# Width transforms in groups of three, and b1 loaded through GpSimd's queue, in a GFNet plus GELU layer

## The chip, the core and the metric

The kernel runs on one core of one Trainium2 chip. The metric is the device time of one execution in microseconds; the time given for a kernel is the median over its runs.

## The reference

An input x of 2048 rows and 640 columns is normalised along its rows. The normalised x feeds two branches, and the input and both branches are added:

```python
def _A_ref(x, w_r, w_i):
    X = rfft2(x.astype(float32), axes=(-2, -1))
    X = X * (w_r + 1j * w_i)
    return irfft2(X, s=(S, D), axes=(-2, -1)).astype(bfloat16)

def _B_ref(x, w1, b1, w2, b2):
    h = gelu(einsum("bsd,df->bsf", x, w1) + b1)      # F = 1536
    return einsum("bsf,fd->bsd", h, w2) + b2

xn = _layernorm(x, axis=-1)
return x + _A_ref(xn, ...) + _B_ref(xn, ...)
```

Branch A is a global filter in the frequency domain, branch B a two-layer perceptron. All tensors are bfloat16.

## The kernel before

**Tiling.** Rows are dealt into 16 blocks of 128 (block c holds every sixteenth row, from row c). The transform over the 2048 rows is split into a transform over the 128 rows of each block (matmuls with the table `gtab`, the "height transforms") and one over the 16 blocks (table `mtab` forward, `ntab` back). The transform over the 640 columns uses symmetries: VectorE folds each row twice (L654, L658), and what is left are four products of 160 columns per block with the table `etab`. On the way back the table is `getab`, and VectorE unfolds twice (L887, L892).

**Stages.** Each stage is a set of operations with the engines they may run on:
- Load x; statistics (L595, L597), reciprocal root on GpSimd (L605), normalise (L619). Blocks 0 to 5 are transposed by TensorE (L631), the others by DMA (L642, on SP's queue).
- First layer of B: for each of seven sets of blocks (`BLOCKS`, 128 to 512 rows wide) and each of twelve chunks of F, five matmuls from `xnT` and W1 into a bank named `hps`, then a gelu on ScalarE (L693), which adds b1 as a column, `b1col`. That column is made from the loaded row of b1 by one matmul (L577) and one copy (L579).
- Forward: the height transforms, evicted to `XW`; then `along_d`, the transforms along the width, for a group of blocks at a time (`BPS`: pair at which the group is issued, first block, number of blocks), evicted to `Xb`, a ring of `NP` blocks; then, for each of eight pairs, the matmuls with `mtab`, evicted to `Y`; the product with the filter on VectorE (`T`, L786; `Z`, L791); small gathers `Zs`; the matmuls with `ntab`, evicted to `XV`.
- Second layer of B for the six `STAGED` blocks, whose sums with b2 are kept in float (L868); for the others it is accumulated in the bank of the final product.
- Back: transforms along the width with `getab` in groups `EPS`, unfolding, then the final matmuls with the table H (kept in `gtab`), the sum with x and b2 (L917) and the store (L920). x is added by accumulating DMAs that GpSimd issues (L906).

**One group of the width transforms** (`five`): each block has four main matmuls on 128 rows of contraction and four remainder matmuls on 32 rows. A group of m blocks issues main matmuls, then all remainders, then the rest of the main ones. A group of three writes two pairs of PSUM banks; a group of four writes a third pair, for its fourth block, and orders two remainders by a semaphore on TensorE itself. Eviction is one copy of 960 columns per pair, and one of 640 for the fourth block.

**Order.** A planner (`Sched.schedule`) walks through time with its own estimates of durations (`five_us`, `IPC` and the like), priorities (`PRIO`), allowed PSUM banks (`ZONE`), and gates, and fixes the order on every engine and queue, the engine of each copy, and the banks. The result is five lists, one for each engine and for SP; each engine runs its list in order and waits on semaphores where the planner found a dependency or a reused buffer. A small change of an estimate or a zone therefore moves many instructions. `QUEUE` is the order of the first loads on SP; `GATE`, `DEPTH` hold later loads back; `PARTS` cuts W1 and W2 by chunks of F: chunks 0 to 2 of W1 go through ScalarE's queue, the others through SP's.

**Lines to know.** Matmuls all carry L491 (transposes L631, the one for b1 L577). Copies from PSUM carry L501 on ScalarE and L504 on VectorE. All loads carry L482. `ps<-etab,XW` is a forward width transform, `ps<-getab,XV` one on the way back, `ps<-Xb,mtab` a forward column group, `ps<-ntab,Z` an inverse one, `ps<-xnT,W` the first layer, `ps<-W,gT` the second, `ps<-Wf,gtab` and `ps<-T,gtab` the final products.

Of the kernel before, what the change touches and what calls it, by code (L numbers as in the profile page):

```python
# [98 lines left out]
def mm_us(n):  # L99
    return max(n / 2400.0 + 0.003, 0.0265)  # L100


def dve_us(n, rate=1.0):
    return 0.066 + n / 960.0 / rate


def act_us(n, ptr=0):
    return 0.052 + n / 1200.0 + 0.092 * ptr
# [3 lines left out]
    return 0.075 + n / 500.0  # L112


ZONE = {'hps': ((4, 8), (0, 4), (2, 8), (2, 8), (0, 4), (4, 8), (0, 8)), 'bps': (0, 8), 'cps': (0, 8), 'dps': (0, 8), 'eps': (0, 6), 'fps': (0, 8), 'fst': (0, 8), 'yps': (0, 2), 'tps': (2, 6), 'aps': (0, 8)}
PRIO = {'hps': 1, 'gelu': 361.0, 'pb': 171.1, 'pc': 177.3, 'filt': 322.7, 'ipc': 497.3, 'xb': 65.8, 'eps': 262.2, 'fin': 110.8, 'fst': 95.7}
BLOCKS = ((0, 1), (1, 2), (2, 4), (4, 6), (6, 9), (9, 12), (12, 16))
AHEAD = 3
STAGED = (0, 2, 4, 6, 8, 10)
XRAT = 4  # L120
LAG = 6
WARM = 11
DEPTH = 5
PACE = 5
BYDMA = (6, 7, 8, 9, 10, 11, 12, 13, 14, 15)
PARTS = (0, 3, 8, 12)
BPS = {0: (0, 4), 1: (4, 4), 3: (8, 4), 5: (12, 4)}
EPS = (0, 3, 6, 10, 13, 16)
NP = 8
W1RATE = 360000.0  # L130
GATE = 2
QUEUE = (('x', 0), ('x', 1), ('w', 1), ('x', 2), ('w', 2), ('x', 6), ('x', 4), ('g', 0), ('x', 10), ('x', 12), ('x', 8), ('x', 14))
XGATE = -16


# [265 lines left out]
def bass_parallel_sum__spectral_gfnet__dense_activation_gelu__prompt_kernel(  # L401
# [17 lines left out]
    b1v = B_b1.rearrange("(c p) -> c p", p=128)  # L419
    b2v = B_b2.rearrange("(o e) -> o e", o=1)  # L420

    K = Sched(nc, ["sp", "pe", "act", "dve", "pool"])
    with ExitStack() as es:
        def sb(name, shape, dtype=BF):
            return es.enter_context(nc.sbuf_tensor(name, shape, dtype))

        def view(t, off, dims):
            width = int(np.prod(t.shape[1:]))
            return bass.AP(tensor=t, offset=off, ap=[[width, 128]] + dims)
# [8 lines left out]
        b1t = sb("b1t", [NFC, 128])  # L438
# [12 lines left out]
        Wf = sb("Wf", [128, WP])  # L451
        xb4 = sb("Xb", [128, 2 * NP * KP])
        Yb = sb("Y", [128, 2, 4 * KP])
# [27 lines left out]
        def load(dst, src, buf, nbytes, after=(), reads=(), rate=330e3, eng="sp", cost=0.46, lat=0.0):  # L481
            return K.op([(eng, cost)], 400 if eng == "act" else 0, lambda e, _: e.dma_start(dst, src), reads=reads, writes=[buf], after=after, nbytes=nbytes, rate=rate, lat=lat)  # L482
# [3 lines left out]
        def mms(lst):  # L486
            def f(e, _):
                for o_, lw, rh, st, sp_, *mark in lst():
                    if mark == ["wait"]:
                        e.wait_ge(fence, len(fences))  # L490
                    ins = e.matmul(o_, lhsT=lw, rhs=rh, start=st, stop=sp_)  # L491
                    if mark == ["signal"]:
                        ins.then_inc(fence, 1)
                        fences.append(ins)
                return ins
            return f
# [12 lines left out]
        K.op([("pool", 0.1)], 100, lambda e, _: e.memset(mhalf[:, 0:8], -0.5), writes=[B_mh])  # L509
        K.op([("pool", 0.1)], 99, lambda e, _: e.memset(view(xb4, KP - 2, [[2 * KP, NP], [1, 3]]), 0.0), writes=[B_xbpad])  # L510
        K.op([("pool", 0.1)], 99, lambda e, _: e.memset(view(xb4, 2 * KP - 1, [[2 * KP, NP], [1, 1]]), 0.0), writes=[B_xbpad])
        wpad = K.op([("pool", 0.1)], 99, lambda e, _: e.memset(view(Wf, 2 * WR, [[1, 2]]), 0.0), writes=[B_wpad])


        B_id, B_b1, B_b2b = Buf("ident"), Buf("b1t"), Buf("b2")
# [12 lines left out]
        def load_w1(j, **how):  # L528
            a, n = PARTS[j], PARTS[j + 1] - PARTS[j]
            load(view(W1, D * a, [[128 * n, 5], [1, 128 * n]]), w1v[:, :, 128 * a:128 * (a + n)], B_w1s[j], 163840 * n, rate=W1RATE, **how)  # L530
# [4 lines left out]
        late_x = []  # L535
        for what, i in QUEUE:
            if what == "x":
# [4 lines left out]
                load(gtab[:].rearrange("p a b -> p (a b)"), const["G"], B_g, 524288)  # L542
        load(ident[:], const["I"], B_id, 32768, eng="act")
        load_w1(0, eng="act")
        load(b1t[:], b1v, B_b1, 3072, eng="act", lat=-3.0)
        few = []

        later = [load(etab[:], const["E"], B_e, 204800), load(mtab[:].rearrange("p a b c d -> p (a b c d)"), const["M"], B_m, 131072),
# [58 lines left out]
        for c in range(16):  # L607
            pr, prf = 100 - c, 100 - c - LAG
            if c % 2 == 0:
# [15 lines left out]
            if c not in BYDMA:  # L625
                for ja, jb, engs in ((0, 5, "da"),) if c > 1 else ((0, 3, "d"), (3, 5, "a")):
                    tps = Buf(f"tps{c}_{ja}", psum, 1, ZONE["tps"])

# [32 lines left out]
            for c in (c - 1, c):  # L661
                aps = Buf(f"aps{c}", psum, 2, ZONE["aps"])
                ring_ops.append(K.op([("pe", 5 * mm_us(128))], prf, mms(lambda c=c, xfv=xfv, aps=aps: [
# [17 lines left out]
        for blk, (c0, c1) in enumerate(BLOCKS):  # L681
            s0, s1 = 128 * c0, 128 * c1
            for fc in range(NFC):
                hps = Buf(f"hps{blk}_{fc}", psum, 1, ZONE["hps"][min(blk, len(ZONE["hps"]) - 1)])
                B_gT[blk, fc] = Buf(f"gT{blk}_{fc}")
                pr = PRIO["hps"] - blk - fc / 20
                part = []
                for js in ((0, 1, 2), (3, 4)):
# [3 lines left out]
                hps_ops.setdefault(blk, []).append(part[0])  # L692
                K.op([("act", act_us(s1 - s0, 1))], pr + PRIO["gelu"], lambda e, _, s0=s0, s1=s1, fc=fc, hps=hps: e.activation(  # L693
                    gT[:, fc, s0:s1], ps(hps.slot, 0, s1 - s0), ACT.Gelu_apprx_tanh, bias=b1col[:, fc:fc + 1], scale=1.0),
# [38 lines left out]
            return PS[buf.slot // 2][:, :].rearrange("p (b n) -> p b n", b=2)[:, :, 0:2 * Q4].rearrange("p b (g k) -> p b g k", g=2)  # L733

        def five_us(m):
            return 4 * m * 0.0695 + m * 0.07 + 0.21
        IPC = 0.78
        pb_ops, filt_ops, cps_ops, t_ops = [], [], {}, {}
        B_v = [Buf(f"v{q}") for q in range(16)]
        B_xb = {}  # L740
# [1 line left out]
        def along_d(i0, m, gate):  # L742

            assert i0 % NP + m <= NP
            bps = [Buf(f"bps{i0}_{v}", psum, 2, ZONE["bps"]) for v in range(2 + m // 4)]
            pr = PRIO["pb"] - i0 / 10
            pb_ops.append(K.op([("pe", five_us(m))], pr, mms(lambda: five(
                bps, lambda g, n: Xa[:, g, i0 + n, :], lambda g, n: Xa[32 * g:32 * g + 32, 4, i0 + n, :], etab, m)),
                reads=B_xa + [B_e], writes=bps, gate=gate))
            free = [o for i in range(max(0, i0 - NP), i0 + m - NP) for o in cps_ops[i // 2]]  # L750
            for i in range(i0, i0 + m):
                B_xb[i] = Buf(f"xb{i}")
            for v in range(2):
                K.op([("dve", dve_us(2 * Q4 * min(m, 3))), ("act", act_us(2 * Q4 * min(m, 3)))], pr,
                     copy(lambda v=v: view(xb4, (i0 % NP) * 2 * KP + v * (KP + 1), [[2 * KP, min(m, 3)], [1, 2], [2, Q4]]),
                          lambda v=v: two(bps[v], min(m, 3))), reads=[bps[v]], writes=[B_xb[i] for i in range(i0, i0 + min(m, 3))], after=free)
# [4 lines left out]
        for pair in range(8):  # L761
            if pair in BPS:
                along_d(BPS[pair][0], BPS[pair][1], cps_ops.get(pair - 2, []))
            Y, TB, Z = Buf(f"Y{pair}", p_y), Buf(f"T{pair}", p_t), Buf(f"Z{pair}", p_z)
            cps = [Buf(f"cps{pair}_{r}", psum, 2, ZONE["cps"]) for r in range(2)]
            cps_ops[pair] = [K.op([("pe", 0.78)], PRIO["pc"] - pair / 5, mms(lambda pair=pair, cps=cps: [
                (ps(cps[r].slot + hi, 0, KP)[64 * qq:64 * qq + 64], mtab[64 * hi:64 * hi + 64, 1 if pair == qq == 0 else 0, v, r, :],
                 view(xb4, (2 * (2 * pair % NP + qq) + v) * KP, [[1, KP]])[64 * hi:64 * hi + 64], v == 0, v == 1)
                for r in range(2) for v in range(2) for hi in range(2) for qq in range(2)]), reads=[B_xb[2 * pair], B_xb[2 * pair + 1], B_xbpad, B_m], writes=cps, gate=t_ops.get(pair - 2, []))]
            for r in range(2):  # L770
                K.op([("act", act_us(644)), ("dve", dve_us(644))], PRIO["pc"] - pair / 5,
                     copy(lambda Y=Y, r=r: view(Yb, Y.slot * 4 * KP + r * KP, [[2 * KP, 2], [1, KP]]),
# [8 lines left out]
            def tv(TB, k, r):  # L781
                return view(TT, TB.slot * 8 * KP + k * 4 * KP + r * KP, [[2 * KP, 2], [1, KP]])
            pr = PRIO["filt"] - pair / 5
            t_ops[pair] = []
# [22 lines left out]
            for n in range(2):  # L807
                gather((128 * n + 31, [[256, 2], [1, 1]]), (KP * n, [[2 * KP, 2], [1, 1]]), 1.0 - 2 * n, tail[n:n + 1], [("dve", 0.07), ("act", 0.06)])
            dps = [Buf(f"dps{pair}_{hi}", psum, 2, ZONE["dps"]) for hi in range(2)]

            def ipc(pair=pair, Z=Z, ZS=ZS, zs=zs, dps=dps):
# [16 lines left out]
                return lst  # L828
            K.op([("pe", IPC)], PRIO["ipc"] - pair / 5, mms(ipc), reads=[Z, ZS, B_n], writes=dps)
            for hi in range(2):  # L830
# [14 lines left out]
        def fin_gate(c):  # L845

            i = rest.index(c)
            return ([fin_ops[rest[i - AHEAD]]] if i >= AHEAD else st_ops[:]) + hps_ops[block_of[c]]

# [15 lines left out]
        for i, c in enumerate(STAGED):  # L865
# [3 lines left out]
                out=halves(view(xnT, 2 * D * i, [[1, 2 * D]]).bitcast(F32)), in0=ps2(fps.slot, H2), in1=halves(b2bc[:]), op=ALU.add), reads=[fps, B_b2b], writes=[B_st2[c]], after=all_hps)  # L869
        for e, (c0, c1) in enumerate(zip(EPS, EPS[1:])):  # L870
            m = c1 - c0
# [24 lines left out]
            for n in range(m):  # L896
# [11 lines left out]
                for pcs in (WHOLE,) if c < 15 else (((0, 0, H2),), ((0, H2, H2 + Q4),), ((0, H2 + Q4, D),)):  # L908
                    a, b = pcs[0][1], pcs[-1][2]
                    os_, fps = Buf(f"os{c}_{a}", p_os), Buf(f"fps{c}_{a}", psum, len(pcs), ZONE["yps" if c in STAGED else "fps"])  # L910
# [42 lines left out]
```

## Time and profile before

| | |
|---|---|
| median of 4 runs | 153.57 us (153.42 to 155.1) |
| the profiled execution | 153.62 us, span of its instructions 151.7 us |
| TensorE busy | 147.1 us, 97% of the span |
| VectorE, ScalarE, GpSimd busy | 114.9, 85.0, 21.0 us |
| granted TensorE clock | 1.0 |
| moved by DMA | 20.81 MB, 137 GB/s over the span |

The profile is one execution. Times in its lines are microseconds from the start of the span; a timeline line gives the start, the time to the end of the last instruction of the row, the engine, the line of the program, the operation, the tiles (out<-in), their shape, the number of instructions, and in brackets the idle time of the engine before the row and what ended it. Ends of matmuls are modelled, so that neighbouring rows overlap; the distance between two starts is what a row costs TensorE. PE is TensorE's matmul, PEld its loading of weights, DVE VectorE, ACT ScalarE, POOL GpSimd.

### The profile page before, as it was taken

How to read it: one execution, taken by the hardware profiler on the slowest of the kernel's cores; microseconds unless marked ns; L12 is line 12 of the kernel's file. 1: busy time of each engine (PE TensorE's matmuls, PEld its weight loads, DVE VectorE, ACT ScalarE, POOL GpSimd, SP SyncE). 2: the span in 40 equal slices, each digit the busy share in tenths (PEclk: the TensorE clock that was granted, in tenths of full speed). 3: DMA queues.
4: the chain of work that ended last, by engine and by line, in shares of the span. 5: the costliest groups of instructions: out<-in, count | busy, mean ns of one | idle time of the engine just before them, and what ended most of it. 6: DMA issues, size and time to landing. Idle time of an engine off the chain costs nothing.

```text
span 151.7 us, 3730 instructions
## 1 busy us (share of the span) xinstructions
PE 147.1 (97%) x1547; PEld 101.6 (67%) x1547; DVE 114.9 (76%) x251; ACT 85.0 (56%) x172; POOL 21.0 (14%) x33
## 2 busy tenths in 40 slices
PE   7899999999999999999999999999999999999993
PEld 2399999956666656546456775677677777777773
DVE  1888999999996599679759838984896597594232
ACT  3297978877778677967974416685403461211000
POOL 1202112110100000000000132058202202212000
PEclk9999999999999999999999999999999999999999
DMA  4999235889697550220605052439955715743511
GB/s 126 367 375 399 98 40 141 190 195 206 104 170 164 102 180 0 57 77 0 201 20 179 0 122 56 86 85 198 236 135 155 194 43 123 192 121 97 139 67 49
DMA packets 20120, 20.81 MB, mean 137 GB/s; under 512 B 8328, under 2 KB 16776, under 8 KB 19976
## 3 DMA queue, kind: packets, MB, share of 16 engines
q1 hardware_dynamic: 16976, 14.81, 36.0%
q0 software_dynamic: 2304, 5.24, 15.8%
q10 hardware_dynamic: 824, 0.53, 1.1%
q8 instruction: 12, 0.20, 0.6%
q14 instruction: 4, 0.03, 0.1%
HBM read 13.69 MB, written 2.62 MB: 108 GB/s over the span
## 4 chain that ended last, share of the span: by engine, by line
PE 85%; ACT 5%; DMA 5%; DVE 2%; SPq 1%; POOL 1%; issue 0%
PE ps L491 84%; DMA XV<-in_A_x_dram 5%; ACT Xb L501 3%; DVE stats L595 1%; ACT gT L693 1%; PE ps L631 1%; SPq L482 1%; ACT XV L501 1%; ACT Zs L501 1%; POOL rstd L605 1%; DVE T L619 0%; DVE T L658 0%; DVE ost L917 0%; DVE mv L597 0%; DVE ve L604 0%
## 5 line engine op out<-in xcount | busy, mean ns | idle before, releaser
L491 PE MATMUL ps<-xnT,W 128*128 128x128 bf16 (+3 forms) x420 | 56.8, 288 | 0.1
L491 PE MATMUL ps<-W,gT 128*128 128x320 bf16 (+1 forms) x396 | 56.9, 295 | 0.0
L491 PEld LDWEIGHTS ps<-W,gT 128*128 128x128 bf16 x396 | 37.4, 98 | 14.4 <-issue 0.5
L491 PEld LDWEIGHTS ps<-xnT,W 128*128 128x128 bf16 x420 | 34.0, 98 | 15.5 <-ACT gT L693 2.9
L693 ACT ACTIVATE gT<-ps,b1col 128x128 bf16<-128x128 f32 (+3 forms) x84 | 40.2, 505 | 6.9 <-PE ps L491 5.6
L501 ACT ACTIVATE XW<-ps 128x640 bf16<-128x640 f32 (+1 forms) x17 | 13.5, 812 | 8.4 <-PE ps L491 8.0
L904 ACT ACTIVATE xo<-b2bc 128x640 f32<-128x640 bf16 x10 | 7.1, 732 | 16.1 <-DVE ost L917 16.1
L595 DVE BATCH_NORM_STATS2 stats<-XV 128x6 f32<-128x320 bf16 x32 | 14.1, 469 | 2.7 <-DMA XV<-in_A_x_dram 2.7
L917 DVE TENSOR_TENSOR ost<-ps,xo 128x640 bf16<-128x640 f32 (+2 forms) x12 | 8.5, 710 | 8.5 <-PE ps L491 8.5
L906 POOL DMA_DIRECT2D xnT<-in_A_x_dram x6 | 6.3, 1050 | 60.9 <-DVE xnT L868 60.9
L504 DVE CAST XW<-ps 128x640 bf16<-128x640 f32 (+1 forms) x10 | 9.2, 922 | 5.6 <-PE ps L491 5.6
L786 DVE TENSOR_TENSOR T<-Y,Wf 128x1288 bf16<-128x1288 bf16 x16 | 12.8, 825 | 0.3
L906 POOL DMA_DIRECT2D xo<-in_A_x_dram x10 | 8.8, 954 | 25.8 <-ACT xo L904 25.7
L501 ACT ACTIVATE Xb<-ps 128x960 bf16<-128x960 f32 (+1 forms) x7 | 7.4, 1096 | 5.9 <-PE ps L491 5.9
L605 POOL TENSOR_TENSOR rstd<-ve,mhalf 128x2 f32<-128x2 f32 (+1 forms) x9 | 6.3, 705 | 31.3 <-DVE ve L604 31.3
L504 DVE CAST Xb<-ps 128x960 bf16<-128x960 f32 (+1 forms) x5 | 5.8, 1174 | 5.0 <-PE ps L491 5.0
L504 DVE CAST XV<-ps 128x640 bf16<-128x640 f32 x8 | 6.6, 821 | 3.6 <-PE ps L491 3.6
L501 ACT ACTIVATE Y<-ps 128x644 bf16<-128x644 f32 x9 | 6.3, 706 | 5.0 <-PE ps L491 4.8
L501 ACT ACTIVATE Zs<-Z 128x128 bf16<-128x128 bf16 (+1 forms) x32 | 6.5, 278 | 2.1 <-DVE Z L791 2.1
L501 ACT ACTIVATE XV<-ps 128x640 bf16<-128x640 f32 x8 | 5.6, 705 | 3.6 <-PE ps L491 3.6
L504 DVE CAST Y<-ps 128x644 bf16<-128x644 f32 x7 | 5.8, 824 | 2.4 <-PE ps L491 2.4
L491 PE MATMUL ps<-getab,XV 128*128 128x160 bf16 (+1 forms) x128 | 7.6, 232 | 0.0
(53 smaller groups left out, 138.9 us busy)
## 6 DMA issues: line engine op xcount, KB each, us to landing
xo<-in_A_x_dram POOLq DMA_DIRECT2D x10, 320.0 KB, 4.6
out_dram<-ost SPq DMA_DIRECT2D x15, 160.0 KB, 2.1
XV<-in_A_x_dram SPq DMA_DIRECT2D x7, 320.0 KB, 9.7
xnT<-in_A_x_dram POOLq DMA_DIRECT2D x6, 320.0 KB, 3.8
W<-in_B_w_dram SPq DMA_DIRECT2D x2, 800.0 KB, 5.8
W<-in_B_w_dram SPq DMA_DIRECT2D x2, 640.0 KB, 6.3
Wf<-in_A_w_r_dram SPq DMA_DIRECT2D x7, 160.5 KB, 3.2
Wf<-in_A_w_i_dram SPq DMA_DIRECT2D x7, 160.5 KB, 4.0
```

The lines of the kernel that those rows point to most:

```text
L482: return K.op([(eng, cost)], 400 if eng == "act" else 0, lambda e, _: e.dma_start(dst, src), reads=reads, writes=[buf], after=after, nbyte ...
L491: ins = e.matmul(o_, lhsT=lw, rhs=rh, start=st, stop=sp_)
L501: return e.activation(dst(), src(), ACT.Copy, scale=scale)
L504: return e.tensor_copy(dst(), src())
L595: K.op([("dve", 0.4)], 100 - c, lambda e, _, c=c, h=h: e.bn_stats(stats[:, c, 6 * h:6 * h + 6], view(XV, c * D + H2 * h, [[1, H2]])), read ...
L605: K.op([("pool", 0.75)], 100 - c, lambda e, _, a=a, b=b: e.tensor_tensor(out=rstd[:, a:b], in0=ve[:, a:b], in1=mhalf[:, 0:b - a], op=ALU.pow),
L631: ins = e.transpose(ps(tps.slot, 0, 512).bitcast(BF)[:, 128 * j:128 * j + 128], xnv(128 * j, [[1, 128]]), ident[:])
L693: K.op([("act", act_us(s1 - s0, 1))], pr + PRIO["gelu"], lambda e, _, s0=s0, s1=s1, fc=fc, hps=hps: e.activation(gT[:, fc, s0:s1], ps(hps. ...
L786: t_ops[pair].append(K.op([("dve", 0.05 + dve_us(4 * KP, 2))], pr, lambda e, _, k=k, Y=Y, TB=TB, pair=pair: e.tensor_tensor(out=view(TT, T ...
L904: K.op([("act", act_us(640))], 30, lambda e, _, xov=xov: e.activation(xov(0, D), b2bc[:], ACT.Copy), reads=[B_b2b], writes=[xi], gate=[z_l ...
L906: K.op([("pool", 1.2)], 50, lambda e, _, c=c, xov=xov: e.dma_start(xov(0, D), xv[:, c, :], accum_op=ALU.add), reads=[xi], writes=[xo], nby ...
L917: os_ops.append(K.op([("dve", dve_us(b - a))], 95, lambda e, _, a=a, b=b, xov=xov, fps=fps, os_=os_: e.tensor_tensor(out=ost[:, os_.slot, ...
```

## The change

The forward width transforms are issued as five groups of three blocks and one group of one (blocks 0-2, 3-5, 6-8, 9-11, 12-14, and 15) instead of four groups of four. The ring of `Xb` holds six blocks instead of eight. On the way back the groups are of 3, 3, 3, 4, 3 blocks instead of 3, 3, 4, 3, 3, so that one group of four is left in the kernel. The row of b1 is loaded by GpSimd's queue instead of ScalarE's, where it stood behind the first part of W1. The planner's priorities, zones and lags are new, its estimates for a group of four and for an inverse group are larger, and two loads of x change places with others in the queue.

```diff
-ZONE = {'hps': ((4, 8), (0, 4), (2, 8), (2, 8), (0, 4), (4, 8), (0, 8)), 'bps': (0, 8), 'cps': (0, 8), 'dps': (0, 8), 'eps': (0, 6), 'fps': (0, 8), 'fst': (0, 8), 'yps': (0, 2), 'tps': (2, 6), 'aps': (0, 8)}
-PRIO = {'hps': 1, 'gelu': 361.0, 'pb': 171.1, 'pc': 177.3, 'filt': 322.7, 'ipc': 497.3, 'xb': 65.8, 'eps': 262.2, 'fin': 110.8, 'fst': 95.7}
+ZONE = {'hps': ((4, 8), (4, 8), (4, 8), (0, 4), (0, 4), (4, 8), (0, 8)), 'bps': (0, 8), 'cps': (0, 8), 'dps': (4, 8), 'eps': (0, 6), 'fps': (0, 8), 'fst': (0, 8), 'yps': (0, 6), 'tps': (0, 4), 'aps': (2, 8)}
+PRIO = {'hps': 50.6, 'gelu': 457.1, 'pb': 105.3, 'pc': 240.1, 'filt': 314.0, 'ipc': 675.1, 'xb': 153.2, 'eps': 335.1, 'fin': 78.1, 'fst': 4.3}
-AHEAD = 3
+AHEAD = 2
-LAG = 6
+LAG = 8
-BPS = {0: (0, 4), 1: (4, 4), 3: (8, 4), 5: (12, 4)}
-EPS = (0, 3, 6, 10, 13, 16)
-NP = 8
+BPS = {0: (0, 3), 1: (3, 3), 2: (6, 3), 4: (9, 3), 6: (12, 3), 7: (15, 1)}
+EPS = (0, 3, 6, 9, 13, 16)
+NP = 6
-QUEUE = (('x', 0), ('x', 1), ('w', 1), ('x', 2), ('w', 2), ('x', 6), ('x', 4), ('g', 0), ('x', 10), ('x', 12), ('x', 8), ('x', 14))
+QUEUE = (('x', 0), ('x', 1), ('w', 1), ('x', 2), ('w', 2), ('x', 6), ('x', 4), ('x', 10), ('g', 0), ('x', 8), ('x', 12), ('x', 14))
...
-        load(b1t[:], b1v, B_b1, 3072, eng="act", lat=-3.0)
+        load(b1t[:], b1v, B_b1, 3072, eng="pool", cost=0.9, lat=-3.0)
...
-            return 4 * m * 0.0695 + m * 0.07 + 0.21
-        IPC = 0.78
+            return 4 * m * 0.0695 + m * 0.07 + (0.32 if m > 3 else 0.21)
+        IPC = 0.82
...
-            cps_ops[pair] = [K.op([("pe", 0.78)], ...
+            cps_ops[pair] = [K.op([("pe", 0.82)], ...
```

What this does to the lists, by the planner's output for both kernels: on TensorE the matmuls are the same in number and shape, and everything up to the transposes of blocks 2 and 3 stands in the same order. The groups of blocks 6-8 and 9-11 are issued back to back, the forward column groups of pairs 3 to 5 follow each other with five first-layer matmuls between them, and the inverse groups of pairs 3 to 7 all come after the last forward one. On SP the transposes of blocks 6 to 11 precede the loads of the tables. On GpSimd one DMA issue is added, between the memsets and the first power.

More of the change, by code (lines that the diff above doesn't have):

```diff
@@ L765, in bass_parallel_sum__spectral_gfnet__dense_activation_gelu__prompt_kernel @@
             cps = [Buf(f"cps{pair}_{r}", psum, 2, ZONE["cps"]) for r in range(2)]
-            cps_ops[pair] = [K.op([("pe", 0.78)], PRIO["pc"] - pair / 5, mms(lambda pair=pair, cps=cps: [
+            cps_ops[pair] = [K.op([("pe", 0.82)], PRIO["pc"] - pair / 5, mms(lambda pair=pair, cps=cps: [
                 (ps(cps[r].slot + hi, 0, KP)[64 * qq:64 * qq + 64], mtab[64 * hi:64 * hi + 64, 1 if pair == qq == 0 else 0, v, r, :],
```

## The prediction

> **What bounds the kernel now.** I read the page first, for the share of each engine over time.
>
> ```profile
> PE 147.1 (97%) x1547; PEld 101.6 (67%) x1547; DVE 114.9 (76%) x251; ACT 85.0 (56%) x172; POOL 21.0 (14%) x33
> PE   7899999999999999999999999999999999999993
> PEclk9999999999999999999999999999999999999999
> ```
>
> TensorE is busy from end to end, at the full granted clock. Its work is fixed, so only two things can move the end: what its instructions cost, and its few waits. Next I read the timeline of TensorE and took the distance from one start to the next (ends are modelled and overlap). First the opening:
>
> ```profile
> 5.77 0.54 PE L631 MATMUL ps<-ident,T 128*128 128x128 bf16 x5
> 6.93 0.18 PE L577 MATMUL ps<-ident,b1t 12*128 12x12 bf16 x1 [0.62 <-DMA b1t<-in_B_b_dram]
> 7.04 0.90 PE L491 MATMUL ps<-xnT,W 128*128 128x128 bf16 x13
> 8.42 4.36 PEld L491 LDWEIGHTS ps<-xnT,W 128*128 128x128 bf16 x78 [0.26 <-DMA W<-in_B_w_dram]
> 9.24 1.28 DVE L595 BATCH_NORM_STATS2 stats<-XV 128x6 f32<-128x320 bf16 x3 [0.34 <-DMA XV<-in_A_x_dram]
> 12.55 0.80 DVE L619 TENSOR_SCALAR T<-XV,mv,rstd 128x640 bf16<-128x640 bf16 x2 [0.46 <-POOL rstd L605]
> 13.06 0.45 PE L631 MATMUL ps<-ident,T 128*128 128x128 bf16 x5
> ```
>
> Three waits stand one behind the other: for b1 until 6.93, for W1's second part until 8.42, for row block 2 (x lands at 9.22, normalised from 12.55) until 13.06. Then the transforms along the width, by group size, with the line that follows each:
>
> ```profile
> 48.91 1.87 PE L491 MATMUL ps<-etab,XW 128*128 128x160 bf16 x32
> 50.61 1.79 PE L491 MATMUL ps<-xnT,W 128*128 128x384 bf16 x10
> 103.67 1.42 PE L491 MATMUL ps<-getab,XV 128*128 128x160 bf16 x24
> 104.92 1.79 PE L491 MATMUL ps<-W,gT 128*128 128x320 bf16 x12
> ```
>
> A group of four takes 50.61 - 48.91 = 1.70 us, a group of three 104.92 - 103.67 = 1.25 us. Last, the waits behind evictions and the row that prices ScalarE's:
>
> ```profile
> 62.98 0.62 PE L491 MATMUL ps<-ntab,Z 64*128 64x128 bf16 x16 [0.22 <-ACT XV L501]
> 75.49 0.45 PEld L491 LDWEIGHTS ps<-ntab,Z 64*128 64x128 bf16 x16 [0.56 <-ACT Zs L501]
> 97.83 0.48 PEld L491 LDWEIGHTS ps<-ntab,Z 64*128 64x128 bf16 x16 [0.34 <-DVE Zs L503]
> 109.54 0.11 PEld L491 LDWEIGHTS ps<-Wf,gtab 128*128 128x128 bf16 x2 [0.27 <-DVE Wf L892]
> 71.45 1.25 ACT L501 ACTIVATE Xb<-ps 128x960 bf16<-128x960 f32 x1 [0.76 <-PE ps L491]
> 72.56 0.67 ACT L693 ACTIVATE gT<-ps,b1col 128x512 bf16<-128x512 f32 x1
> ```
>
> Against the same steps elsewhere in the trace, where nothing waits (0.09 us from the last 128-row matmul to an inverse group), these four lose 0.28, 0.14, 0.11 and 0.10 us: 0.63 us. That is all of TensorE's avoidable waiting after 13.06, and so nearly all that rearranging can win. (1.0% of this kernel, 1.5 us, is about what a measurement can tell from no change.)
>
> **The sum** starts from the profiled execution: 153.62 us, span 151.7; the median of the runs shown is 153.57, so no correction is needed.
>
> *b1 on GpSimd's queue: 0.* GpSimd's last memset starts at 0.87, so the issue starts near 1.0; an accumulating issue in this trace occupies it 0.87 us, so it is free by 1.9, long before its first pow at 4.72, and no pow is late. Landing: the 32 KB identity takes 2.4 us, GpSimd's own 320 KB transfers 3.8 and 4.6 us, so b1 lands between 3.4 and 5.6; the transposes ahead of it start at 5.77 in either case. The wait for b1 goes. What is late next is W1's second part: only 15 matmuls (three chunks of F) can run without it, and it lands at 8.42 whatever b1 does; behind that, block 2 holds 13.06. TensorE gets to both waits about 0.35 us sooner and waits that much longer. Cover gone would mean both landing earlier, and nothing ahead of them in SP's queue is removed. Bounds: 0 to -0.1 us (78 matmuls from 8.42 end at 12.95, 0.1 short of 13.06). b1 could even land as late as 7.1: 15 matmuls at 0.056 and five transposes still fit before 8.42. ScalarE loses the 0.74 us issue; its table load ends 0.7 sooner, at 3, and its next work is at 6.35. The Trainium skill ("DMA: Bandwidth & Descriptors", Anatomy of one DMA, SWDGE path) gives a fixed 2.0 us for a transfer from GpSimd, an estimate of 3.0 for landing, and lists the path as slower to its first byte than ScalarE's, which speaks against the move; by either, the sum stays at 0.
>
> *Groups by three: 0.* Four groups of four (4 x 1.70 = 6.82) become five of three and one of one. The three: 5 x 1.25 = 6.25. No row shows a group of one. Carrying the step from three to four (0.45) down gives 1.25 - 0.90 = 0.34, the low bound. From its pieces: four 128-row matmuls at 0.069 = 0.28, plus the change to 32-row matmuls and back, 0.10 + 0.16 in the group of three, plus 0.02 for the four small ones = 0.56, the value taken, since the piece rows are of the same instructions. High bound: 0.28 plus all the 0.60 that a group of four has besides its 128-row matmuls, 0.88. Sum 6.81: -0.01, between -0.23 and +0.31. The inverse groups only swap places (3,3,4,3,3 to 3,3,3,4,3). The skill ("TensorEngine Tiling (Array Packing)", Key Properties) says that a change of tiling mode drains TensorE, against cutting groups up; by that rule alone, two more groups at 0.26 would cost +0.5.
>
> *Evictions:* 10,240 float columns through ScalarE and VectorE as before, twelve copies as before. What moves is which engine does them and what PSUM they hold: a group of three holds four banks of eight, a group of four held six. So I walked the new order of the queues, with starts in this trace as prices (512-wide matmul 0.216; forward column group 0.68, inverse 0.67; ScalarE: Xb 1.10, Y 0.60, gelu of 512 0.56, small Zs 0.15; VectorE: Xb 1.14, Y and XV 0.74, two T 1.49, two Z 0.83; 0.15 from an end to who waits). The old three waits at inverse groups go, -0.28 - 0.14 - 0.11 = -0.53; the wait of 0.10 ahead of the first final matmul has the same neighbours and stays. New waits:
> 1. Groups (6..8) and (9..11) now run back to back and fill all eight banks; the next matmul of block 6 takes the pair that ScalarE empties. From the end of pair 2's forward matmuls (0): Y by ScalarE, which has Zs ahead of it, to 1.05; T to 2.65; XV to 3.4; Z to 4.2; ScalarE's Zs to 4.8; its Xb to 5.9; bank free 6.05. TensorE: 7 matmuls 1.6, inverse 0.67, five 1.08, two groups 2.50 = 5.85. Wait 0.20.
> 2. The second staged product starts in a pair that group (12..14) held, evicted wholly by ScalarE: from that group's end, Y of pair 5 to 0.3, Xb to 1.4, gelu to 1.95, three Zs to 2.35, Xb to 3.45, free 3.6. TensorE comes at 0.43 + 12 x 0.136 + 0.56 + 4 x 0.136 = 3.2. Wait 0.4, and 0.05 for the first staged product, in the pair of pair 5's Y.
> 3. Blocks 0 to 2 now share four banks (before: four each, then six). ScalarE's gelu runs at 0.30 a chunk against 0.28 on TensorE; it falls 1 to 2 chunks back, less than four, except at the first 256-wide chunk and the second height transform: 0.05 each, 0.1.
>
> +0.2 + 0.45 + 0.1 = +0.75, each from 0 to twice that. *SP's order, 0.* x 10 ahead of G delays G by 0.9 to about 15, needed at 16.8. Six transposes instead of two now precede the tables, so the same transposes and filter loads follow in another order; the first transpose waits for a normalisation that VectorE reaches 1.1 us later (about 21.6 for 20.5). The last filter issue ends at 49.6 in this trace, 3.6 us to land: 53.2, at worst 54.3 after; its first reader starts at 54.05, in my walk at 54.15, and what VectorE has behind it (the second Xb) is needed 0.3 us after it can be done. So 0, and up to +0.5.
>
> Sum: 153.62 + 0 - 0.01 - 0.53 + 0.75 = 153.83, say **153.8 us**.
>
> **Rivals.** (A) *The relief is real.* The old waits go, and the new order's do not come (my hops of 0.15 and ScalarE's order are the weak points): 153.62 - 0.53 = 153.1, and 152.9 with the cheap group of one. For it: half the kernel's banks free beside a group. Against: ScalarE still runs in order, and Xb of 1.10 sits ahead of gelus and banks.
> (B) *Slower: VectorE's chain of the last five pairs.* All forward matmuls now come before the inverse groups of pairs 3 to 7, which follow each other at 1.85, 2.4, 2.4 and 3.5 us: 10.1 us of TensorE from the third to the seventh. Behind it VectorE has four XV (2.9), three pairs of Z (2.5), two T (1.5), two staged sums (1.5) and Zs (0.4) = 8.8 us, and two-deep Z buffers tie it to TensorE. Margin 1.3, less hops some 0.6. If VectorE comes there more than 0.6 us late (pair 6's Y waits for ScalarE's last Xb), each further microsecond is paid; 2 us late, as a pair's T and XV queued the wrong way round would make it, gives 153.8 + 1.4 = 155.2. For: VectorE is 76% busy, and 4.1 us a pair against 2.4. Against: it idles about 1.4 us before pair 6 in my walk.
> (C) *The filter arrives late.* SP waits in its new order for rows 14 and 15, and twelve filter loads, 0.73 us each, stand behind them. Every 0.1 us beyond 54.4 costs 0.1; landing at 55.5 gives 153.8 + 1.1 = 154.9. Against: those rows are normalised at about 38, and 38 + 2 x 1.3 + 12 x 0.73 = 49.4.
>
> **How the numbers follow.** Forecast (waits only move) 0.58, A 0.25, B 0.11, C 0.06. The forecast's own range is 153.2 to 154.6 (new waits 0.1 to 1.5). A reaches 152.8 (0.1 below its cheap end, for b1); B and C reach 155.2. Range 152.8 to 155.1. Faster than 152.03 takes more than all the waits that TensorE has: 0.04 out of A and 0.01 of the forecast. Slower than 155.11: 0.08 of B and 0.03 of the rest. Within 1%: 0.84.
>
> **What would show it.** After: the b1 matmul starts at about 6.35 and the 78 matmuls still at 8.4, the transposes of block 2 still at 13.06; groups of three 1.25, of one 0.56; a wait of 0.2 on ScalarE's Xb after the 48 matmuls, and of 0.4 ahead of the second staged product; none above 0.1 before an inverse group. Wrong would be: W1's second part or block 2 earlier, inverse groups of pairs 3 to 7 waiting on VectorE, the first filter product waiting on a load, or TensorE's total of starts changing by over 0.3 us without a wait.

## The result, and the profile after

| | before | after |
|---|---|---|
| median of the runs | 153.69 us (56 runs, 153.35 to 155.52) | 154.49 us (35 runs, 154.05 to 156.17) |
| ratio of after to before | | 1.0044, 95% interval 1.0027 to 1.0062 |
| the profiled execution | 153.62 us, span 151.7 us | 155.69 us, span 153.5 us |
| the same kernel profiled once more (e1) | | 154.34 us, span 152.2 us |

The changed kernel is slower by 0.4% (0.3% to 0.6%): 0.7 us, inside the 1% that was called no change. Both kernels have some executions that are more than 1 us longer, at a mean granted clock of 0.989 (by their times 11 of the 56 before and 2 of the 35 after, so that the others differ by more, 153.62 against 154.48 in the median, 0.86 us), and the profiled execution of after is one of them (last section). Therefore the opening is read in a second profile of the same kernel, e1 below, and the rest in both.

The page of after, its rows of TensorE:

```profile
PE 147.9 (96%) x1547; PEld 102.6 (67%) x1547; DVE 114.8 (75%) x250; ACT 85.6 (56%) x173; POOL 21.6 (14%) x34
PE   7599999999999999999999999999999999999993
PEclk9969999999999999999999999999999999999999
```

The second slice of the upper row (5) and the third of the lower one (6) are the long opening. Behind them TensorE is as full as before: these digits can't show where 0.7 us went, and the starts on TensorE must.

The timeline of TensorE, opening, in the second profile of the changed kernel (e1):

```profile
5.77 0.54 PE L631 MATMUL ps<-ident,T 128*128 128x128 bf16 x5
6.25 0.18 PE L577 MATMUL ps<-ident,b1t 12*128 12x12 bf16 x1
6.79 0.90 PE L491 MATMUL ps<-xnT,W 128*128 128x128 bf16 x13 [0.37 <-ACT xnT L501]
7.81 4.84 PE L491 MATMUL ps<-xnT,W 128*128 128x128 bf16 x80
8.11 4.36 PEld L491 LDWEIGHTS ps<-xnT,W 128*128 128x128 bf16 x78 [0.21 <-DMA W<-in_B_w_dram]
12.76 0.45 PE L631 MATMUL ps<-ident,T 128*128 128x128 bf16 x5
```

The wait for b1 is gone: its matmul starts at 6.25 instead of 6.93, and ScalarE's copy of `xnT` comes next. In this execution W1's second part lands about 0.3 us sooner than in the profile of before (8.11 for 8.42), and block 2's transposes follow at 12.76 instead of 13.06.

The timeline of TensorE in after: the width transforms, the waits, and an inverse group.

```profile
50.59 1.42 PE L491 MATMUL ps<-etab,XW 128*128 128x160 bf16 x24
51.85 1.95 PE L491 MATMUL ps<-xnT,W 128*128 128x384 bf16 x10
...
67.16 2.67 PE L491 MATMUL ps<-etab,XW 128*128 128x160 bf16 x48
70.08 1.90 PE L491 MATMUL ps<-xnT,W 128*128 128x512 bf16 x8 [0.25 <-ACT Xb L501]
71.91 0.62 PE L491 MATMUL ps<-ntab,Z 64*128 64x128 bf16 x16
...
82.69 0.63 PE L491 MATMUL ps<-etab,XW 128*128 128x160 bf16 x8
83.25 0.72 PE L491 MATMUL ps<-W,gT 128*128 128x320 bf16 x4
84.33 0.72 PE L491 MATMUL ps<-W,gT 128*128 128x320 bf16 x4 [0.36 <-ACT Xb L501]
```

A group of three takes 51.85 - 50.59 = 1.26 us, the group of one 83.25 - 82.69 = 0.56. No inverse group waits: start to start, each of the eight comes when the matmuls ahead of it are through (70.08 + 8 x 0.216 + 0.09 = 71.90 for 71.91). Instead two waits on ScalarE's `Xb` stand at 70.08 and 84.33. The bracket gives idle time against modelled ends; start to start, against the same matmuls elsewhere, they cost 0.41 and 0.52 us. Three smaller ones are new as well: 0.10 us ahead of the second forward column group at 59.38, 0.07 ahead of the first staged product at 81.01, and 0.04 ahead of the group of one at 82.69.

ScalarE's timeline in after, ahead of each of the two:

```profile
68.17 0.71 ACT L501 ACTIVATE Zs<-Z 128x128 bf16<-128x128 bf16 x4
68.78 2.35 ACT L501 ACTIVATE Xb<-ps 128x960 bf16<-128x960 f32 x2
...
81.94 0.69 ACT L693 ACTIVATE gT<-ps,b1col 128x512 bf16<-128x512 f32 x1
82.50 0.63 ACT L501 ACTIVATE Zs<-Z 128x128 bf16<-128x128 bf16 x3
83.00 1.66 ACT L501 ACTIVATE Xb<-ps 128x960 bf16<-128x960 f32 x2
```

In both places the copy that frees the banks stands behind small `Zs` and starts when TensorE is nearly there: 68.78 for a matmul that could start at 69.67 (70.08 - 0.41), 83.00 for one that could at 83.81 (84.33 - 0.52). One copy of 960 columns takes 1.1 us.

### The profile page after: what moved, and what is told of

Its sections match the earlier page's. It is cut to its first block, busy times and chain, and to the rows that moved or that the text cites. A ratio compares the mean times of both kernels' runs of the same rounds, so it can differ in the third digit from the quotient of the medians.

```text
span 153.5 us, 3730 instructions
## 1 busy us (share of the span) xinstructions
PE 147.9 (96%) x1547; PEld 102.6 (67%) x1547; DVE 114.8 (75%) x250; ACT 85.6 (56%) x173; POOL 21.6 (14%) x34
## 4 chain that ended last, share of the span: by engine, by line
PE 82%; ACT 7%; DVE 6%; DMA 2%; issue 0%; SPq 0%; DVEq 0%
PE ps L491 80%; DMA XV<-in_A_x_dram 2%; ACT Xb L501 2%; DVE T L786 2%; ACT Zs L501 2%; PE ps L631 1%; ACT Y L501 1%; DVE Z L791 1%; ACT gT L693 1%; ACT XV L501 1%; DVE Xb L504 1%; DVE stats L595 1%; DVE Y L504 1%; DVE XV L504 0%; ACT xnT L501 0%
## 5 line engine op out<-in xcount | busy, mean ns | idle before, releaser
L491 PE MATMUL ps<-xnT,W 128*128 128x128 bf16 (+3 forms) x420 | 58.2, 294 | 0.6 <-ACT xnT L501 0.4
L491 PEld LDWEIGHTS ps<-xnT,W 128*128 128x128 bf16 x420 | 35.4, 101 | 15.8 <-ACT gT L693 2.1
L501 ACT ACTIVATE XW<-ps 128x640 bf16<-128x640 f32 (+1 forms) x15 | 11.9, 807 | 8.0 <-PE ps L491 7.9
L504 DVE CAST XW<-ps 128x640 bf16<-128x640 f32 (+1 forms) x12 | 11.2, 932 | 4.0 <-PE ps L491 3.9
L906 POOL DMA_DIRECT2D xo<-in_A_x_dram x10 | 9.6, 991 | 21.4 <-ACT xo L904 21.4
L501 ACT ACTIVATE Y<-ps 128x644 bf16<-128x644 f32 x10 | 7.0, 707 | 4.3 <-PE ps L491 4.3
L504 DVE CAST Y<-ps 128x644 bf16<-128x644 f32 x6 | 5.0, 826 | 4.8 <-PE ps L491 4.8
L501 ACT ACTIVATE XV<-ps 128x640 bf16<-128x640 f32 x9 | 6.2, 696 | 3.9 <-PE ps L491 3.9
L504 DVE CAST XV<-ps 128x640 bf16<-128x640 f32 x7 | 5.7, 817 | 2.5 <-PE ps L491 2.5
L491 PE MATMUL ps<-etab,XW 128*128 128x160 bf16 (+1 forms) x128 | 7.6, 233 | 0.0
```

Source lines behind the costliest of these rows:

```text
L501: return e.activation(dst(), src(), ACT.Copy, scale=scale)
L504: return e.tensor_copy(dst(), src())
L906: K.op([("pool", 1.2)], 50, lambda e, _, c=c, xov=xov: e.dma_start(xov(0, D), xv[:, c, :], accum_op=ALU.add), reads=[xi], writes=[xo], nby ...
```

## The experiments

A measure used throughout: the time on TensorE from the transposes of block 2 to the start of the last matmul. It leaves out the opening, which differs between executions of one kernel. Before it is 136.01 us, in the profile of after 136.63.

| run | median, us | ratio to before, 95% | block 2 to last matmul, us |
|---|---|---|---|
| e1, the change again | 154.43 | 1.0057 (1.0042 to 1.0071) | 136.83 |
| e2, before, b1 on GpSimd's queue | 153.47 | 0.9987 (0.9975 to 0.9998) | 136.00 |
| e3, after, b1 on ScalarE's queue | 154.57 | 1.0061 (1.0045 to 1.0076) | 136.96 |
| e4, after, blocks 12-14 evicted by two engines | 154.24 | 1.0035 (1.0013 to 1.0056) | 137.23 |
| e5, after, filter loads ahead | 154.27 | 1.0042 (1.0022 to 1.0062) | 136.66 |
| e6, e4 and e5 together | 153.91 | 1.0003 (0.9975 to 1.003) | 136.22 |
| e7, e6 and two groups set apart | 152.86 | 0.9926 (0.9897 to 0.9955) | 135.45 |
| e8, before, groups of three alone | 155.35 | 1.0122 (1.007 to 1.0174) | 137.65 |

(The runs of before beside e1 to e4 had a median of 153.60 us, those beside e5 to e8 153.66.)

**e1, the change again**, no edit.

> The changed kernel once more, unchanged, for its usual opening: the execution profiled first has a clock of 0.989 and row block 2's transposes 1.24 us later than before, and 155.69 us against a median of 154.49. Theory W (the change is waits in the middle): 154.4 to 154.6; the three waits of 0.1, 0.4 and 0.5 us (second forward column group, after the 48 matmuls, second staged product) stand again, 0.57 us more than before in sum; what is left of the difference to before, about 0.2 us, is in the opening, where the transposes of block 2 start at 13.1 to 13.4. Rival S (the opening does most of it): the transposes of block 2 start at 13.6 or later in an ordinary execution too, and the middle adds less than 0.3.

The two waits return to the hundredth, 0.41 and 0.52 us, and the median is the one that theory W expected. Two things are not as it said: block 2's transposes start at 12.76, sooner than in the profile of before, so that no part of the loss is in this opening; and the wait at the second column group, 0.10 us in the profile of after, is larger. VectorE's timeline in e1, at the first product with the filter:

```profile
52.99 0.83 DVE L504 CAST Y<-ps 128x644 bf16<-128x644 f32 x1 [1.22 <-PE ps L491]
54.22 1.57 DVE L786 TENSOR_TENSOR T<-Y,Wf 128x1288 bf16<-128x1288 bf16 x2 [0.39 <-DMA Wf<-in_A_w_i_dram]
55.82 0.90 DVE L791 TENSOR_TENSOR Z<-T 128x644 bf16<-128x644 bf16 x2
56.64 1.24 DVE L504 CAST Xb<-ps 128x960 bf16<-128x960 f32 x1
```

and TensorE's, at the column group that needs that `Xb`:

```profile
55.44 2.38 PE L491 MATMUL ps<-xnT,W 128*128 128x384 bf16 x12
58.03 0.74 PE L491 MATMUL ps<-Xb,mtab 64*64 64x322 bf16 x16 [0.21 <-DVE Zs L504]
```

The filter is late, VectorE waits, and `Xb` behind it in VectorE's list makes TensorE wait 0.28 us (of which 0.11 stands without a late filter, see e5). The bracket names `Zs`, a neighbour in VectorE's list; what had to be done is the `Xb` ahead of it. This is rival C in small. In the profile of after, TensorE and VectorE come there 1.54 us later than in e1, but the last filter issue ends only 1.22 us later (51.76 for 50.54), and the load was just in time.

**e2 and e3, b1 alone and everything but b1.** e2 is before with the second line, e3 is after with the first.

```diff
-        load(b1t[:], b1v, B_b1, 3072, eng="act", lat=-3.0)
+        load(b1t[:], b1v, B_b1, 3072, eng="pool", cost=0.9, lat=-3.0)
```

> The kernel before with only b1's row moved to GpSimd's queue; all five lists are otherwise those of before. Theory W: no change, within 0.1 us of before (b1's wait goes, W1's second part is waited for until 8.4 instead). Rival Q (GpSimd's DMA delays the first loads, or the earlier table load does): 0.2 to 0.4 us slower, with x's second block or W1's second part landing later by as much.

> The changed kernel with b1's row back on ScalarE's queue behind W1's first part; the other lists are those of the changed kernel. Theory W: 154.5, as the changed kernel, with the b1 matmul at about 6.9. Rival Q: 0.2 to 0.4 us faster than the changed kernel.

The timeline of TensorE in e2:

```profile
6.17 0.18 PE L577 MATMUL ps<-ident,b1t 12*128 12x12 bf16 x1
...
8.75 4.53 PE L491 MATMUL ps<-xnT,W 128*128 128x128 bf16 x78 [0.75 <-DMA W<-in_B_w_dram]
13.39 0.45 PE L631 MATMUL ps<-ident,T 128*128 128x128 bf16 x5
```

b1's matmul starts 0.76 us sooner than before, and the same time is spent waiting for W1's second part, which lands at 8.75. e2's interval allows a gain of 0.03 to 0.4 us; the edit made the other way round, e3 against e1, costs 0.14 us, and the intervals of those two overlap. So b1's move gains 0 to 0.4 us, more likely near 0.15; the landing of W1's second part alone varies by more (8.1 in e1, 8.42 before, 8.75 here), so no single profile can show it. Both came out as theory W had it, but for e2's median, 0.13 us below before and so 0.03 outside its 0.1; rival Q has nothing for it. The slowdown is not b1's: e3 has it in full.

**e4, the eviction of blocks 12 to 14 by two engines.** The two 960-column copies of this group go one to VectorE and one to ScalarE, instead of both to ScalarE.

```diff
-[("dve", ...), ("act", ...)]
+[("dve", ...), ("act", ...)][v:v + 1] if i0 == 12 else [("dve", ...), ("act", ...)]
```

> The changed kernel with one eviction moved: of the group of blocks 12 to 14, the second pair of banks is copied by VectorE instead of ScalarE (and one of the two small copies of block 15 by ScalarE instead). Everything planned up to there is the same. Theory W: the wait of 0.5 us ahead of the second staged product goes and nothing takes its place: 154.0. Rival V (VectorE is as full): the copy comes late there too, or the filter products behind it do, and the wait comes back at the next column or inverse groups: 154.5.

The timeline of TensorE in e4, where the second staged product's four matmuls are the last of the row of twelve:

```profile
82.79 1.97 PE L491 MATMUL ps<-W,gT 128*128 128x320 bf16 x12
84.69 0.74 PE L491 MATMUL ps<-Xb,mtab 64*64 64x322 bf16 x16
```

The wait ahead of that product falls from 0.52 to 0.16 us (it lies inside the row now), and no wait takes its place at a later column or inverse group. Yet in this profiled execution the filter was later still, and the whole stage longer. VectorE's timeline in e4, and the column group on TensorE:

```profile
53.04 0.83 DVE L504 CAST Y<-ps 128x644 bf16<-128x644 f32 x1 [1.22 <-PE ps L491]
55.12 1.57 DVE L786 TENSOR_TENSOR T<-Y,Wf 128x1288 bf16<-128x1288 bf16 x2 [1.26 <-DMA Wf<-in_A_w_i_dram]
...
58.93 0.74 PE L491 MATMUL ps<-Xb,mtab 64*64 64x322 bf16 x16 [1.07 <-DVE Zs L504]
```

It cost TensorE 1.14 us there. The median of all its runs, 154.24, fell by 0.2 us against e1 (intervals overlap) and lies between the 154.0 of theory W and the 154.5 of rival V: the relief is seen in the trace, not in this time alone. Its twelve runs spread from 153.58 to 154.81, 1.2 us, where e1's six spread 0.6.

**e5, the filter loads ahead.** `GATE` 2 to 0. Only SP's list changes: the tables and five filter loads stand ahead of transposes that they followed.

```diff
-GATE = 2
+GATE = 0
```

> The changed kernel with GATE 0 instead of 2: on SP the four tables and the first five filter loads go out ahead of the first transposes; the lists of the other four engines are those of the changed kernel. Theory F (part of the loss is the filter's arrival: the first filter product waits 0.4 to 1.3 us for a load in three of four profiles of the changed order, and the second forward column group with it, 0.1 to 1.1 us): that wait goes, the second column group starts with its usual 0.09 us, and the median falls by about 0.3, to 154.1, with less scatter between runs. Rival W0 (the wait is there but a later one has the same end): 154.4 as before.

SP's queue, its last row of filter loads: in before,

```profile
45.75 3.83 SPq L482 DMA_DIRECT2D Wf<-in_A_w_i_dram  x5
```

in after and in e1,

```profile
47.23 4.53 SPq L482 DMA_DIRECT2D Wf<-in_A_w_i_dram  x5
46.00 4.54 SPq L482 DMA_DIRECT2D Wf<-in_A_w_i_dram  x5
```

in e5,

```profile
41.54 2.56 SPq L482 DMA_DIRECT2D Wf<-in_A_w_i_dram  x4
```

The last issue ends at 49.6 in before, 51.8 in after, 50.5 in e1 and 44.1 us in e5. In e5 the first filter product no longer waits (54.02, no bracket), and TensorE's wait at the column group is 0.11 us, as in e6 and e7. That rest isn't a load: `Y`, the two products, `Z` and `Xb` follow each other on VectorE without a gap. The two waits on ScalarE remain (0.41 and 0.53). The median is 0.16 us below e1's, about the 0.17 by which this wait shrank there; by their intervals alone the two times are the same. The 0.3 that theory F expected did not come, nor the smaller scatter: the runs spread over 0.77 us. So that the load makes the time vary is seen in the traces of e1, e3 and e4, not in the spread of the times.

**e6 and e7, taking the causes away one after the other.** e6 joins e4 and e5. e7 also lets the group of blocks 9 to 11 wait for the column group of pair 3, so that it no longer follows the group of 6 to 8 directly:

```diff
-                along_d(BPS[pair][0], BPS[pair][1], cps_ops.get(pair - 2, []))
+                along_d(BPS[pair][0], BPS[pair][1], cps_ops.get(pair - (1 if pair == 4 else 2), []))
```

> GATE 0 and the eviction of blocks 12 to 14 divided between ScalarE and VectorE. Theory W+F: both waits go, and the 0.4 us after the 48 matmuls stays: 154.43 - 0.3 - 0.45 = 153.7, the same as before within 0.15. Rival V (VectorE gives it back before the last inverse groups): 154.1, as with GATE 0 alone.

> As the run before, and the group of blocks 9 to 11 held until pair 3's column group starts, so that the two groups of 48 matmuls no longer follow each other and never fill all eight banks; the order behind it is planned anew (some products of the second layer earlier). Theory W+F: the wait of 0.4 goes as well: 153.3, 0.2 to 0.3 below before. Rival (two-deep Y and Z buffers: with the column groups moved, a new wait of the same size appears at a column or inverse group): 153.7.

e6 comes out at 153.91, e7 at 152.86 us: e6 is 0.2 above what theory W+F expected, e7 0.4 below. The timeline of TensorE in e6:

```profile
65.86 2.67 PE L491 MATMUL ps<-etab,XW 128*128 128x160 bf16 x48
68.79 1.90 PE L491 MATMUL ps<-xnT,W 128*128 128x512 bf16 x8 [0.25 <-ACT Xb L501]
```

and in e7:

```profile
65.75 1.42 PE L491 MATMUL ps<-etab,XW 128*128 128x160 bf16 x24
67.01 1.89 PE L491 MATMUL ps<-xnT,W 128*128 128x512 bf16 x8
...
72.45 1.42 PE L491 MATMUL ps<-etab,XW 128*128 128x160 bf16 x24
73.71 1.67 PE L491 MATMUL ps<-xnT,W 128*128 128x512 bf16 x7
```

The two groups now stand 6.7 us apart with an inverse and a column group between, and the matmuls behind both start without a wait. In e7 none of the waits is left but the 0.11 at the column group. Its 152.86 us is below both kernels, 0.5% to 1.0% below before. Its books close: without the old waits (0.53, and 0.10 at the first final product) and with 0.11 new, TensorE should need 136.01 - 0.52 = 135.49 from block 2 to the end, and needs 135.45. In e6 the wait at the first final product is gone too; three waits listed above (0.11, 0.41, 0.16) and two small ones, 0.07 at the first staged product and 0.05 ahead of the group of one, make 136.18 of its 136.22. In e7 these two went with the new order, which is why it gained more than the 0.41 aimed at. The rest of e7's gain on before, 0.8 us in the medians, lies ahead of block 2 (12.88 for 13.06 in the profiles); whether that is b1's move or the opening's variation isn't shown.

**e8, the groups alone.** `BPS` and `NP` of after in before, all priorities and zones as before:

```diff
-BPS = {0: (0, 4), 1: (4, 4), 3: (8, 4), 5: (12, 4)}
+BPS = {0: (0, 3), 1: (3, 3), 2: (6, 3), 4: (9, 3), 6: (12, 3), 7: (15, 1)}
-NP = 8
+NP = 6
```

> The kernel before with the forward groups alone changed (3, 3, 3, 3, 3, 1 blocks, ring of six), with its own priorities, banks, loads, and groups on the way back; the planner orders the rest anew. If groups of three cost nothing in themselves, TensorE's starts add up to those of before less 0.01 us, a group of one takes 0.56, and the time differs from before only by waits that can be named: 153.4 to 154.2. Rival (cutting up costs the changes of mode): 0.5 us more on TensorE without any wait, 154.1 or more.

The timeline of TensorE in e8:

```profile
61.24 1.42 PE L491 MATMUL ps<-etab,XW 128*128 128x160 bf16 x24
...
63.05 0.28 PE L491 MATMUL ps<-ntab,Zs 64*128 64x64 bf16 x8
63.99 0.82 PE L491 MATMUL ps<-xnT,W 128*128 128x512 bf16 x3 [0.66 <-ACT Xb L501]
...
76.71 1.88 PE L491 MATMUL ps<-etab,XW 128*128 128x160 bf16 x32
79.62 1.25 PE L491 MATMUL ps<-xnT,W 128*128 128x512 bf16 x5 [1.03 <-ACT Xb L501]
```

The matmuls of a group cost here what they cost elsewhere. What costs is the same wait as in after, but larger: 0.73 and 1.10 us start to start, and 0.26 after two groups in a row at 49.12. (At 76.71 the planner put the groups of 12 to 14 and of 15 together.) The time, 155.35 us, is over both the 154.2 expected and the rival's 154.1, but it is waits that make it so: without the old 0.63 and with these, TensorE should need 136.01 - 0.63 + 2.09 = 137.47 us from block 2 to the end, and needs 137.65. So the rest of the change taken together (priorities, zones, lags, the loads, the groups on the way back) takes more than half of this back: with it the groups of three come out 0.7 us above before, without it 1.7. Which part of it does so was not run.

## Why the prediction was right, and which terms were off

The predicted time was 153.8 us, the measured 154.49: no change by the bound that the text set, on the slow side as the sum had it, inside the range and near the upper end of the forecast's own (154.6). The mechanism held: the old waits go, and new ones on ScalarE's order come. The sizes were too small: the sum had a loss of 0.2 us. Step by step:

- **b1, 0 us: right.** b1's matmul at 6.25 (predicted 6.35), and the time went into the wait for W1's second part (e2). GpSimd's issue started at 1.36 and occupied it 0.68 us, later than the estimate of 1.0 but far from its first pow at 4.73. If there is a gain, it is 0.15, slightly past the bound of 0.1. The arrival of W1's second part was taken as fixed at 8.42; it is 8.1 to 8.75.
- **Groups by three, -0.01: right.** 1.26 for a three, 0.56 for the one. The value from its pieces, 0.56, is what was measured. The drain at a change of tiling is inside these figures; at 0.26 a group on top, as the weighed rule would have it, the new groups would take 0.5 us more than the old ones, and they take 0.04 (5 x 1.26 + 0.56 = 6.86 for 4 x 1.70 = 6.82 before, by rounded rows).
- **Old waits, -0.53: right.** All three are gone in every profile of the new order, and no inverse group waits on anything. The wait of 0.10 ahead of the first final product stays (108.17 in after).
- **Term (1), 0.20: the place and the cause right, the size 0.41.** The walk's TensorE side was right to 0.04 us (69.67 for 69.63). ScalarE's was 0.25 late (70.08 for 69.83): `Z` on VectorE ends 0.1 later, four `Zs` instead of a lump of 0.6, a copy of 1.15 and not 1.10. Most steps of this chain were priced a little below what they take, and the errors add, since the wait is the difference of two sums of 6 us.
- **Term (2), 0.4 and 0.05: 0.52 and 0.07.** ScalarE's `Zs` took 0.50 for 0.40, and the hop to TensorE 0.23 for 0.15. e4 shows the cause: half of the copies to VectorE, and 0.36 of the 0.52 goes.
- **Term (3), 0.1: none seen.** Four banks for blocks 0 to 2 are enough.
- **SP's order, 0 with up to +0.5: mis-sized.** This is the step that failed. It took the last filter issue to land at 54.3 at worst, the reader at 54.15, and 0.3 us of margin behind it, and so costed nothing. The margin isn't there: with the load in time the column group still waits 0.10 (after) or 0.11 us (e5), for VectorE's own chain. And the load can be late: the reader is ready at about 53.9 when the opening is ordinary, the last issue ended at 50.5 in e1, and TensorE lost 0.28 there, 0.43 in e3, 1.14 in e4. So it is a wait between 0.1 and 1.1 us that changes from execution to execution. Rival C, held at 0.06, was no rival to the forecast but a part of it.

With these, for e1: -0.53 + 0.41 + 0.52 + 0.07 + 0.28 = +0.75 us, and TensorE took 136.83 - 136.01 = +0.82 from block 2 to its last matmul. For the profile of after, with 0.10 in place of 0.28, +0.57 and +0.62. The sum had +0.75 of new waits; there are 1.28 of them in e1, 0.35 more than foreseen in its terms (1) and (2), 0.28 at the column group behind the loads, less 0.1 for term (3).

**Its own signs of being wrong.** Two of them came. The first filter product waits on a load, as said. And block 2 is earlier in e1, 12.76 for 13.06; in e2 it is later, 13.39, so this moves by 0.3 us either way between executions, and the text had taken it as fixed. The other two did not come: no inverse group of pairs 3 to 7 waits on VectorE, and TensorE's total is explained by named waits to within 0.1 us.

**Rival A** (the relief is real) fell on ScalarE's order, as the text said against it; e7 shows that its time, 153.1, was to be had, and a little more, with three edits to the order. **Rival B** (VectorE's last five pairs) fell: the inverse groups of pairs 3 to 7 lose only the 0.10 us at their start that they lose wherever nothing waits.

## What to carry to other kernels

Here, with TensorE full, cutting a step into other groups changed its own price by 0.04 us at most; what it changed is which copy frees which bank, and when. For every place where two groups stand back to back, or where a group's copies all fall to one engine, write down when the next user of those banks arrives and when the last copy ends, with what stands ahead of that copy in its engine's list. And a load whose margin is 0.1 us is not a cost of nothing: here it cost between 0 and 1 us.

## What the runs showed of the hardware

**TensorE's clock fell after an idle time of 1.2 us.** The timeline of TensorE in the profile of after, opening:

```profile
1.06 3.90 PE L491 MATMUL ps<-gT 128*128 128x512 bf16 x11 [1.06 <-DVE gT L568]
6.18 0.54 PE L631 MATMUL ps<-ident,T 128*128 128x128 bf16 x5 [1.22 <-DVE T L619]
...
7.19 1.55 PE L491 MATMUL ps<-xnT,W 128*128 128x128 bf16 x13 [0.37 <-ACT xnT L501]
...
14.30 0.44 PE L631 MATMUL ps<-ident,T 128*128 128x128 bf16 x5
```

and its table of stretches, in which the number after GpSimd's busy time (POOL) is the granted clock (PEclk):

```profile
core 0: us, PE busy (x) PEld busy (x) DVE busy (x) ACT busy (x) POOL busy (x), PEclk, DMA share, GB/s
7.00:8.00 1.00, 0.81 (x8) 0.81 (x9) 0.61 (x2) 0.28 (x3) 0.32 (x1) 0.62 1.03 385
8.00:9.00 1.00, 1.00 (x12) 1.00 (x11) 0.33 (x1) 0.67 (x2) 0.00 (x0) 0.50 1.08 381
...
10.00:12.00 2.00, 2.00 (x33) 2.00 (x31) 2.00 (x7) 1.75 (x6) 0.00 (x0) 0.83 1.06 392
```

The eleven warm-up matmuls were done at 4.96 us (they took 3.90 us here, 4.57 in e1), x's second block was late, and TensorE stood for 1.2 us. By these rows the granted clock was 0.5 from about 7.3 to 10.7 (0.62 over 7 to 8 and 0.83 over 10 to 12 place the two ends); thirteen matmuls took 1.55 us instead of 0.90, and block 2's transposes started 1.24 us later than in the profile of before. The stretch of 3.4 us is the length of the window that the Trainium skill gives ("TensorE: Matmul & The Clock Gate", Part 1: The HAM clock gate), which also says that the window runs freely. It puts the fall after a whole idle window; here, in the 3.41 us ahead of the fall (3.85 to 7.26), TensorE was busy for 1.82, so that about half of one was idle. This is one profile, and nothing was run on it: that warm-up by number of matmuls, not by time, is what lets it happen is argued, not shown.

**Loads behind one another in a queue vary by a microsecond.** The last five filter loads took 4.53, 4.54, 4.13 and 5.59 us to issue in after, e1, e3 and e4, which share SP's list, and 3.83 in before at the end of another. What they shared the DMA engines with was not looked into.
